# Attention and two MLPs on one core: late weight pairs in two parts beside the attention, the distance table's scaling behind a softmax, two sets of output tiles

## Chip, cores and metric

The kernel runs on one core of one Trainium2 chip. The metric is the device time of one launch in microseconds (us). Before the change it is 1016.96 us, the median of three runs (1013.14 to 1026.87). The profiled execution that all rows here come from took 1018.65 us, with a span of 1016.9 us inside it.

## What is computed

The reference is one attention layer with a learned bias on the distance, followed by two MLPs on all 2304 tokens (4 batches of 576). All data are float32.

```python
scores = q @ k.T / sqrt(64)                      # 4 batches, 8 heads, 576 x 576
x = log1p(abs(i - j)) / log1p(max(i, 1))         # the distance table
bias = relu(x * w1 + b1) @ w2                    # 32 hidden, one value per head
attn = softmax(scores + bias); a = attn @ v      # a: 2304 x 512
h = max(a @ w1, a @ w2, a @ w3)                  # first MLP, 512 -> 768
y = h @ w_out                                    # 768 -> 512
g = h2 if h2 >= 1 else 0 if h2 <= -1 else (h2 + 1)**2 / 4,  h2 = y @ w_in   # 512 -> 2048
out = g @ w_out2                                 # 2048 -> 512
```

## The kernel before

**Numbers.** Almost every product on TensorE (PE) is made of float16 halves: a float32 tensor is scaled by a power of two and split into a high and a low float16, and three products (high by high, high by low, low by high) are summed. So each weight has to be prepared once: the MLP weights come in as 64-bit floats, and `decode` (L457) turns a raw tile into float32 bits by two ScalarE (ACT) instructions (L462 writes a tile `z` from the high words, L463 writes `y` from the low words), one VectorE (DVE) instruction (L464, z = z shifted, or y) and one more ACT instruction (L465, a bfloat16 copy of |z| for the scale). `pair_scale` (L543) sums the columns of that copy over partitions with eight matmuls against ones on PE (L549) for a pair of tiles, and DVE takes the maximum and makes a power of two of it (L552, L136, L137, L141). `split` (L154) then writes the high half on ACT (L157) and the low half on DVE (L158). `decode` may be given a tile for z or, with None, makes z in place in the high words of the raw tile, that is with a step of two words; the first MLP's weights do so (L491), the late ones are given a tile of the pool `sp` (L579).

**Stages.** The work is cut into 144 slots, one for a block of 128 query rows, a batch and a head (or two heads for the short last block): 96 slots for the first three row blocks, then 48 in which the short block 4 and block 3 alternate for each batch. A slot is: the scores on PE (L691, into the pool `s` of two PSUM tiles), their sum with the bias and the row extreme on DVE (L705, into `sp`, a pool of four tiles), the exponential on ACT (L707), a float16 high half on ACT (L723), a low half on GpSimd (POOL; L724, L725, which end the use of the `sp` tile), a DMA transpose from SP's queue (L727), and three slots later the product with v on PE (L747, L743). A finished batch of a block is normalised (L756 to L762) and transposed into `xT` (L770). Between these, the main loop (L924) puts matmuls of the first MLP (mlp1, L802, with L807 and L809 on its results, and mlp2, L824) at a rate per slot, so that PE has work while a softmax runs. mlp2 scales its PSUM result into a tile of the pool `hl` on ACT (L829; two tiles), takes a maximum on DVE (L830) and stores it to DRAM from SP's queue (L831).

**Bias tables.** While a row block runs, the bias of the next is built in groups (L382 and L363): masks on DVE (L389, L369), matmuls (L393, L373), and a sum with the distance table. The distance table comes from DRAM by a DMA (L297, L302) at the start of a block, and `xscale` (L305) multiplies it by a column on DVE (L307). `new_xt` (L908) calls xscale at a table's first use; there are four such calls.

**Late weights.** The weights of the second MLP are the "late" pieces (L556): 16 pairs of tiles, by turns two of w_in and two of w_out, taken by a generator that is advanced by `late_to` (L538). Two advances make one pair: today all of the pair is done in the first one (the load of the next tile, both decodes, the load of the one after, the sums, the splits), and the second does nothing. The raw tiles of the first five pairs rotate over three places in `ws`, and tile x + 3 takes the place of tile x. During the last 48 slots the generator is advanced 0.3 times a slot (L983), up to ten advances, so five pairs (N_BIAS = 10 tiles) fall beside the attention; the others come after it, beside the rest of the first MLP.

**After the attention.** `wide` is set (L926) when the slots are at an end; from then on mlp1 and mlp2 may use the PSUM pool `s` too. The rest of the first MLP runs; then the second MLP for row block 0 (h2_mm L1041, g_mid L1047, out_mm L1067), beside which POOL prepares combinations of the output weights (wcomb L1096 to L1111); then the second MLP for the other blocks (h2_half L1119, g_pair L1125, out7 L1158) to the end.

**What sets the order.** The program is written in one order, and a scheduler reorders the instructions of each engine by priority and by its own estimate of the times, within the data's dependencies. `tc.issue_after(x)` forbids it to put an instruction ahead of x. `last_pair[0]` is the latest softmax's DVE instruction (L705) or, before the first softmax, the last bias instruction. On the chip each engine runs its instructions in the order that results, and so does SP's DMA queue.

Of the kernel before, what the change touches and what calls it, by code (L numbers as in the profile page):

```python
# [9 lines left out]
F32 = mybir.dt.float32  # L10
U32 = mybir.dt.uint32
# [9 lines left out]
def kernel(ctx: ExitStack, tc: tile.TileContext, qt, kt, vr, small, mw1, mw2, mw3, mwo, win, wo2, out):  # L21
# [8 lines left out]
    P = 128  # L30
    B, H, S, D = 4, 8, 576, 64
# [61 lines left out]
    def st(shape, dt, tag):  # L93
        return sb.tile(shape, dt, tag=tag, name=tag, bufs=BUFS.get(tag, 1))
# [59 lines left out]
    def split(hi, lo, src, scale, eng):  # L154

        if eng == "v":
            A.activation(hi, src, AF.Copy, scale=scale)  # L157
            V.scalar_tensor_tensor(lo, src, scale, hi, ALU.mult, ALU.subtract)  # L158
        else:
            G.tensor_tensor(src, src, (scale.unsqueeze(2) if len(src.shape) == 3 else scale).to_broadcast(src.shape), ALU.mult)  # L160
            A.activation(hi, src, AF.Copy)
            G.tensor_tensor(lo, src, hi, ALU.subtract)

    if True:
# [65 lines left out]
        wide, halves_left, turn = [], [], [0]  # L230
# [74 lines left out]
        def xscale(j, t):  # L305

            V.tensor_scalar(t, t, ipsi[:, j:j + 1], None, ALU.mult)  # L307
# [99 lines left out]
        last_pair = [None]  # L407
# [41 lines left out]
        def raw_load(src, r):  # L449
            SP.dma_start(r if len(src.shape) == 2 else r.rearrange("p (k f) -> p k f", k=src.shape[1]), src)  # L450
            return r
# [5 lines left out]
        def decode(r, z, y):  # L457

            w = r.bitcast(U32).rearrange("p (n two) -> p n two", two=2)
            if z is None:  # L460
                z = w[:, :, 1]
            A.activation(z.bitcast(F32), w[:, :, 1].bitcast(F32), AF.Prelu, scale=-(2.0 ** -80), alpha=-(2.0 ** -32))  # L462
            A.activation(y, w[:, :, 0], AF.Copy, scale=2.0 ** -29 * (1 - 2.0 ** -20), bias=-0.5)  # L463
            V.scalar_tensor_tensor(z, z, 3, y, ALU.logical_shift_left, ALU.bitwise_or)  # L464
            A.activation(high(y), z.bitcast(F32), AF.Abs)  # L465
            return z.bitcast(F32)

        def high(y):

            return y.bitcast(BF16)[:, 0:512]  # L470
# [55 lines left out]
        N_BIAS = 10  # L526

        def late_home(x):
            if x == 10:
                home[10] = st([P, S], F32, "xtab").bitcast(F16)[:, :1024]  # L530
            while len(home) <= x:
                home.append((st([P, S], F32, "k").bitcast(F16) if len(home) < 32 else st([P, 9, P], F16, "pt").rearrange("p c k -> p (c k)"))[:, :1024])
            return home[x]
# [22 lines left out]
        def late_pieces():  # L556

            spec = []
            for ft in range(0, NF2, 2):
                spec.append([win[:, P * f:P * f + P].rearrange("(k p) f -> p k f", p=P) for f in (ft, ft + 1)])  # L560
                spec.append([wo2[P * f:P * f + P, :] for f in (ft, ft + 1)])

            spec = sum(spec, [])

            def load(x):
                if x >= len(spec):
                    return
                r = [raws[:, 0], raws[:, 1], rt_.rearrange("p a c -> p (a c)").bitcast(I64)][x % 3]
                if x >= N_BIAS + 2 and x % 3 < 2:
                    r = st([P, 10, 256], F16, "v").rearrange("p a c -> p (a c)")[:, 0:2048].bitcast(I64)  # L570
                loaded.append(raw_load(spec[x], r))

            loaded = []
            load(0)
            load(1)
            for y in range(len(spec) // 2):
                load(2 * y + 2)
                dst = [late_home(2 * y + i) for i in range(2)]
                zs = [decode(loaded[2 * y + i], st([P, S], F32, "sp")[:, :512].bitcast(U32), dst[i].bitcast(U32)) for i in range(2)]  # L579
                load(2 * y + 3)  # L580
                q = y // 2
                s = c_sq2[:, q:q + 1] if y % 2 else c_sp[:, 2 * q:2 * q + 2]
                pair_scale(s, [d.bitcast(U32) for d in dst], 12 if y % 2 else 14)
                for i in range(2):
                    split(dst[i][:, 0:512], dst[i][:, 512:1024], zs[i], s[:, 0:1] if y % 2 else s[:, i:i + 1], PENG[y % 2])
                yield
                yield

        wo_done, n_wo = [], [0]
# [48 lines left out]
        def load(key):  # L638
            if key in kbox:
                return  # L640
            kind, j, b = key[:3]
            i0, n = BLK[j][0], BLK[j][1]
            if kind == "q":

                t = qz[:, key[3] % 4]
                if j == SJ:
                    for x in range(2):
                        p = slice(64 * x, 64 * x + 64)
                        G.memset(t[p, :, 64 - 64 * x:128 - 64 * x], 0.0)
                        SP.dma_start(t[p, :, p], qt[b, :, p, i0:i0 + n].rearrange("c p i -> p c i"))  # L650
                else:
                    SP.dma_start(t, qt[b, :, :, i0:i0 + n].rearrange("c p i -> p c i"))
            elif kind == "k":
                t = st([P, S], F32, "k")
                SP.dma_start(t, kt[b, key[3]])
            else:
                t = st([P, 10, 256], F16, "v")
                SP.dma_start(t, v_d[b, key[3]])
            kbox[key] = t
# [156 lines left out]
        def mlp2(key, d):  # L816
            while not wo_done:
                n_wo[0] += 1
                next(pieces, None)
            pm = mlp_ps()[:, :256]  # L820
            hh = hhs[:, order_of(key) % 2]
            for ft in range(NF1):
                for y, (wp, hp) in enumerate(SPLIT3):
                    T.matmul(pm, wo16[:, ft, wp, P * d:P * d + P], hh[:, ft, hp], start=(ft == 0 and y == 0), stop=(ft == NF1 - 1 and y == 2))  # L824
            t = st([P, 256], F32, "hl")
            bs = range(B) if key[0] == SJ else (2 * key[1], 2 * key[1] + 1)
            for x, b in enumerate(bs):
                c = slice(256 // len(bs) * x, 256 // len(bs) * (x + 1))
                A.activation(t[:, c], pm[:, c], AF.Copy, scale=c_rb[:, b:b + 1])  # L829
            V.tensor_reduce(c_xm[:, key[0], 4 * key[1] + d:4 * key[1] + d + 1], t, AX.X, ALU.max, apply_absolute_value=True)  # L830
            SP.dma_start(x2_d[key[0]][:, d, 256 * key[1]:256 * key[1] + 256], t)  # L831
# [74 lines left out]
        xts, scaled = {}, set()  # L906

        def new_xt(j):  # L908
            if j not in scaled:
                scaled.add(j)  # L910
                xscale(j, xts[j])
            return xts[j]

        early = {}
# [266 lines left out]
        for x in range(len(work) + GL):  # L1181
            if x < len(work):
                y, sub, ft = work[x]
# [17 lines left out]
            if x >= GL:  # L1201
                y, sub, ft = work[x - GL]
# [48 lines left out]
```

## Time and profile before

| | |
|---|---|
| median of three runs | 1016.96 us (1013.14 to 1026.87) |
| the profiled execution | 1018.65 us, span 1016.9 us |
| PE busy | 932.2 us of the span, 92% |
| DVE, ACT, POOL busy | 702.2, 600.9, 511.4 us |
| attention | ends about 557 us into the span |
| last 317 us | the second MLP, blocks 1 to 4 |

[...] In rows of a timeline, "[2.39 <-ACT ab L465]" says that the engine stood idle for 2.39 us before this instruction and that the ACT instruction of line 465, which wrote `ab`, ended the wait. [...]

### The profile page before, as it was taken

Reading aid. Unit: us, or ns where it says so; the run is one execution under the profiler, and the core shown is the slowest. Engines: PE = TensorE matmul, PEld = TensorE weight load, DVE = VectorE, ACT = ScalarE, POOL = GpSimd, SP = SyncE. Lnnn points to the kernel's source line nnn. Section 1 sums busy time; section 2 is a strip of 40 time slices with the busy share of each in tenths; the row PEclk is TensorE's granted clock in tenths of the full one; section 3 lists DMA queues with packets and bytes.
Section 4 is the critical chain, followed back from the end, with each engine's and each line's share of the span. In section 5 each row is a group of like instructions: output and inputs, shape, how many; then the busy total and the mean of one; then the engine's idle time right before and its main releaser. Section 6 shows DMA issues by size and latency. Waiting matters only on the chain. (4 is left out here: it accounts for less than half of the span.)

```text
span 1016.9 us, 25952 instructions
## 1 busy us (share of the span) xinstructions
PE 932.2 (92%) x10258; PEld 759.5 (75%) x10258; DVE 702.2 (69%) x1551; ACT 600.9 (59%) x1194; POOL 511.4 (50%) x734
## 2 busy tenths in 40 slices
PE   6776788899999999999889888989999999999996
PEld 5555668688888878777677777534588888888885
DVE  8976978777656686556455477886686686586565
ACT  4778975865666545778577689543344454444342
POOL 4131478666876755646357112977044343444442
PEclk9776969999999999999999999989999999999999
DMA  9877999999998979999989753010020010000000
GB/s 296 251 246 132 241 199 247 201 246 188 234 226 203 182 181 210 212 226 229 204 173 199 186 198 127 22 42 1 1 84 22 1 43 19 5 22 11 12 22 22
DMA packets 238970, 141.47 MB, mean 139 GB/s; under 512 B 187520, under 2 KB 217728, under 8 KB 238336
## 3 DMA queue, kind: packets, MB, share of 16 engines
q1 hardware_dynamic: 238688, 139.55, 58.3%
q8 instruction: 80, 1.31, 0.5%
q14 instruction: 42, 0.34, 0.1%
q10 hardware_dynamic: 160, 0.26, 0.1%
HBM read 79.68 MB, written 15.27 MB: 93 GB/s over the span
## 5 line engine op out<-in xcount | busy, mean ns | idle before, releaser
L802 PEld LDWEIGHTS <-aw 128*128 128x128 f16 x2160 | 190.0, 99 | 45.4 <-issue 23.4
L802 PE MATMUL pm<-xT,aw 128*128 128x256 f16 (+1 forms) x1812 | 202.7, 264 | 6.4 <-ACT hl L829 2.9
L725 POOL TENSOR_TENSOR phl<-sp,phl 128x512 f16<-128x512 f32 x136 | 161.6, 1189 | 0.0
L707 ACT ACTIVATE sp<-sp,mx 128x576 f32<-128x576 f32 x144 | 110.6, 768 | 69.9 <-DVE mx L705 69.4
L724 POOL TENSOR_TENSOR phl<-sp,phl 128x64 f16<-128x64 f32 x136 | 49.5, 364 | 179.2 <-ACT phl L723 145.6
L691 PE MATMUL s<-k,qz 64*128 64x288 f32 (+1 forms) x576 | 128.3, 460 | 10.4 <-DVE mx L705 7.9
L705 DVE CUSTOM_DVE_ANT_0 sp<-s,ab 128x576 f32<-128x576 f32 x128 | 93.2, 751 | 32.3 <-PE s L691 10.4
L1136 ACT ACTIVATE sp<-pm,vec 128x256 f32<-128x256 f32 x112 | 61.4, 556 | 81.2 <-PE pm L1119 78.1
L747 PEld LDWEIGHTS <-pt 128*128 128x128 f16 x1792 | 73.7, 101 | 30.5 <-DMA pt<-phl 20.3
L691 PEld LDWEIGHTS s<-k,qz 64*128 64x128 f32 (+1 forms) x576 | 70.4, 201 | 29.1 <-DVE mx L705 9.7
L723 ACT ACTIVATE phl<-sp 128x576 f16<-128x576 f32 x136 | 89.8, 672 | 3.5 <-DMA pt<-phl 2.6
L747 PE MATMUL pav<-v,pt 128*128 128x64 f16 x1568 | 72.1, 198 | 16.0 <-DMA pt<-phl 15.8
L1140 POOL TENSOR_TENSOR hh<-hh 128x128 f32<-128x128 f32 x56 | 33.0, 590 | 106.3 <-DVE hh L1138 90.2
L1119 PEld LDWEIGHTS <-ab 128*128 128x128 f16 x756 | 73.8, 98 | 9.2
L1137 DVE SCALAR_TENSOR_TENSOR hh<-pm,vec,sp 128x256 f32<-128x256 f32 x112 | 52.4, 477 | 33.5 <-ACT sp L1136 33.2
L824 PE MATMUL pm<-hh,wo 128*128 128x256 f16 x558 | 69.0, 273 | 2.6 <-POOL hh L814 1.0
L824 PEld LDWEIGHTS <-wo 128*128 128x128 f16 x648 | 61.0, 98 | 13.4 <-issue 6.1
L814 POOL TENSOR_TENSOR hh<-hm,hh 128x256 f16<-128x256 f32 (+1 forms) x60 | 44.8, 747 | 51.6 <-ACT hh L813 50.3
L1158 PEld LDWEIGHTS <-xT 128*128 128x128 f16 x588 | 57.5, 98 | 7.8 <-ACT xT L1145 1.2
L1158 PEld LDWEIGHTS <-wo 128*128 128x128 f16 x588 | 57.5, 98 | 6.7
L809 DVE SCALAR_TENSOR_TENSOR hm<-pm,hm 128x256 f32<-128x256 f32 (+1 forms) x108 | 41.9, 389 | 27.6 <-PE pm L802 10.6
L1141 POOL TENSOR_TENSOR hh<-hh 128x128 f32<-128x128 f32 x56 | 26.3, 470 | 68.5 <-DVE hh L1138 66.3
(300 smaller groups left out, 2004.4 us busy)
## 6 DMA issues: line engine op xcount, KB each, us to landing
k<-in_k_dram SPq DMA_DIRECT2D x64, 288.0 KB, 3.7
v<-v_d SPq DMA_DIRECT2D x24, 640.0 KB, 4.9
ws<-in_moe_w_out_dram SPq DMA_DIRECT2D x15, 512.0 KB, 5.0
ws<-in_moe_w_in_dram SPq DMA_DIRECT2D x9, 512.0 KB, 5.4
x_d<-hl SPq DMA_DIRECT2D x36, 128.0 KB, 2.5
qz<-in_q_dram SPq DMA_DIRECT2D x16, 256.0 KB, 5.0
ab<-in_moe_w_dram SPq DMA_DIRECT2D x8, 512.0 KB, 9.5
qz<-x_d SPq DMA_DIRECT2D x4, 1024.0 KB, 4.8
```

The source lines that it names most:

```text
L691: last_score[0] = T.matmul(sbox[i + r][:, c, :288], q[p, s if u.j == SJ else s // 2], k[p, 288 * c:288 * c + 288], start=True, stop=True)
L705: last_pair[0] = V.tensor_tensor_reduce(halves(sn), sbox.pop(i)[:, :, :288], halves(bias_sb[u.j][:, h]), -0.125, 3e38, ALU.add, ALU.min, mx)
L707: last_soft[0] = A.activation(pf, sn, AF.Exp, scale=-1.0, bias=mx, accum_out=u.sums[:, h:h + 1])
L723: A.activation(hl[:, :S], pf, AF.Copy)
L725: G.tensor_tensor(hl[:, S + 64:], pf[:, :512], hl[:, :512], ALU.subtract)
L747: T.matmul(u.pav[:, 64 * h:64 * h + 64], pt[:, c], v[:, sl, 64 * (h % 4):64 * (h % 4) + 64], **kw)
L802: T.matmul(o, wm[:, ft, i, wp, kk], x_rhs(key, xp, kk) if n == 256 else x_rhs(key, xp, kk)[:, c], start=(x == 0), stop=(x == 11))
L824: T.matmul(pm, wo16[:, ft, wp, P * d:P * d + P], hh[:, ft, hp], start=(ft == 0 and y == 0), stop=(ft == NF1 - 1 and y == 2))
L1119: T.matmul(pm, w[:, wp, kk], x2t[ORDER[y]][:, kk, xp, 256 * sub:256 * sub + 256], start=(x == 0), stop=(x == 11))
L1136: A.activation(r, pm, AF.Relu, scale=c_ch[:, f], bias=c_half)
L1137: V.scalar_tensor_tensor(t, pm, c_c[:, f], r, ALU.mult, ALU.max)
L1158: T.matmul(m[x], gl[:, gp, i], w[:, wp], start=(start and z == 0 and x % 2 == 0), stop=(stop and z == 2 and (x % 2 == 1 or x == 6)))
```

## The change

Three edits. First, in `late_pieces`, the pairs whose tiles all lie beside the attention (y = 0 to 4, `two`) are decoded in place, with no tile of `sp`, and are cut in two: the first advance makes the load of the next tile and the two decodes, the second makes the sums, the scale, the splits and then the load of the tile after, which used to come ahead of the sums. Since z now lies in the raw tile, that place is free for tile x + 3 only after the split has read it. Second, xscale is put after the latest softmax by `issue_after`. Third, while `wide` is set, every second output of mlp2 takes a tile of the pool `btmp` (two tiles, used in the bias stage and by `all_max`) in place of `hl`. The later lines move by 7, from L912 on by 8.

```diff
@@ late_pieces
             for y in range(len(spec) // 2):
                 load(2 * y + 2)
                 dst = [late_home(2 * y + i) for i in range(2)]
-                zs = [decode(loaded[2 * y + i], st([P, S], F32, "sp")[:, :512].bitcast(U32), dst[i].bitcast(U32)) for i in range(2)]
-                load(2 * y + 3)
+                two = 2 * y + 1 < N_BIAS
+                zs = [decode(loaded[2 * y + i], None if two else st([P, S], F32, "sp")[:, :512].bitcast(U32), dst[i].bitcast(U32)) for i in range(2)]
+                if two:
+                    yield
+                else:
+                    load(2 * y + 3)
                 q = y // 2
                 s = c_sq2[:, q:q + 1] if y % 2 else c_sp[:, 2 * q:2 * q + 2]
                 pair_scale(s, [d.bitcast(U32) for d in dst], 12 if y % 2 else 14)
                 for i in range(2):
                     split(dst[i][:, 0:512], dst[i][:, 512:1024], zs[i], s[:, 0:1] if y % 2 else s[:, i:i + 1], PENG[y % 2])
-                yield
+                if two:
+                    load(2 * y + 3)
+                else:
+                    yield
                 yield
@@ mlp2
-            t = st([P, 256], F32, "hl")
+            t = st([P, 256], F32, "btmp" if wide and d % 2 else "hl")
@@ new_xt
-                xscale(j, xts[j])
+                with tc.issue_after(last_pair[0].ins):
+                    xscale(j, xts[j])
```

PE's order around the second late pair, beside the attention. Before, the first four matmuls of the sum (L549) stand behind a product with v (L747) and ahead of the first MLP's matmuls (L802):

```order
L747 LDWEIGHTS pt
L747 MATMUL pav<-v,pt 128x64
L549 LDWEIGHTS ones
L549 MATMUL pm<-ab,ones 128x128
L549 LDWEIGHTS ones
L549 MATMUL pm<-ab,ones 128x128
L549 LDWEIGHTS ones
L549 MATMUL pm<-ab,ones 128x128
L549 LDWEIGHTS ones
L549 MATMUL pm<-ab,ones 128x128
L802 LDWEIGHTS aw
L802 MATMUL pm<-xT,aw 128x256
```

With the change, all eight stand together, behind that MLP work and one more pair of scores (L809 is the former L802; shown are the end of that work and the first two of the eight):

```order
L809 LDWEIGHTS aw
L809 MATMUL pm<-xT,aw 128x256
L809 LDWEIGHTS aw
L809 MATMUL pm<-xT,aw 128x256
L549 LDWEIGHTS ones
L549 MATMUL pm<-ab,ones 128x128
L549 LDWEIGHTS ones
L549 MATMUL pm<-ab,ones 128x128
```

Twelve such matmuls of the MLP stand between the last scores and the sum there, and two more rounds of twelve have moved ahead of it. The sum has gone from the place where its input has just been asked for to one about a slot later.

SP's queue near the end of the first late pair (names in brackets are the semaphores waited for; L450 is a load of a raw weight tile, L727 a transpose for the softmax, L770 one of a normalised block, L831 a store of mlp2). Before, both loads stand far up and wait for ACT, that is for the decodes:

```order
L658 DMA v<-v_d 128x2560 [waits PE_49]
L450 DMA ws<-in_moe_w_out_dram 128x512 [waits DMAHW7_49,Activation_49]
L655 DMA k<-in_k_dram 128x576 [waits DMAHW0_49,PE_49]
L450 DMA ws<-in_moe_w_in_dram 128x4x128 [waits DMAHW1_49,Activation_49]
L727 DMA_TRANSPOSE pt<-phl 128x9x128 [waits DMAHW2_49,Activation_49,Pool_49]
L770 DMA_TRANSPOSE xT<-px 128x8x128 [waits DMAHW3_49,Pool_49]
```

With the change (L734, L777, L662 and L838 are the former L727, L770, L655 and L831):

```order
L734 DMA_TRANSPOSE pt<-phl 128x9x128 [waits DMAHW0_49,PE_49,DMAHW6_49,Activation_49,Pool_49]
L777 DMA_TRANSPOSE masks<-px 128x4x128 [waits DMAHW7_49,Pool_49]
L450 DMA ws<-in_moe_w_out_dram 128x512 [waits DVE_49]
L662 DMA k<-in_k_dram 128x576 [waits DMAHW1_49,PE_49]
L450 DMA ws<-in_moe_w_in_dram 128x4x128 [waits DMAHW2_49,DVE_49]
L838 DMA x_d_75<-hl 128x256 [waits DMAHW3_49,Activation_49]
L734 DMA_TRANSPOSE pt<-phl 128x9x128 [waits DMAHW4_49,PE_49,Pool_49]
```

Both loads now wait for DVE, the split, and stand seven transposes (two of them of normalised blocks) and two loads of k lower.

DVE's order at the short block's distance table (`ws`). Before, its scaling stands in the middle of block 3's bias groups:

```order
L399 TENSOR_TENSOR btmp<-pm,xtab 128x256
L389 TENSOR_TENSOR masks<-rw,thr 128x1024
L400 SCALAR_TENSOR_TENSOR ab<-pm,vec,btmp 128x8x32
L307 TENSOR_SCALAR ws<-ws,vec 128x288
L389 TENSOR_TENSOR masks<-rw,thr 128x1024
L399 TENSOR_TENSOR btmp<-pm,xtab 128x256
```

With the change it stands directly ahead of its first use (L376), behind a softmax (L712, the former L705):

```order
L712 ISA sp,mx<-s,ab 128x576
L712 ISA mx 128x1
L307 TENSOR_SCALAR ws<-ws,vec 128x288
L816 SCALAR_TENSOR_TENSOR hm<-pm,hm 128x256
L369 TENSOR_TENSOR masks<-rw,thr 128x1024
L816 SCALAR_TENSOR_TENSOR hm<-pm,hm 128x256
L376 TENSOR_TENSOR btmp<-pm,ws 128x256
```

The first table's scaling moves in the same way, 88 rows down DVE's order, and between there and the end of block 1's bias groups the scheduler has dealt all engines a somewhat different order.

## Rows read from the trace of the kernel before

**Rows 1.** The page, part 1: span and busy time of each engine.

```profile
span 1016.9 us, 25952 instructions
PE 932.2 (92%) x10258; PEld 759.5 (75%) x10258; DVE 702.2 (69%) x1551; ACT 600.9 (59%) x1194; POOL 511.4 (50%) x734
```

**Rows 2.** Windows by stage: busy per engine, then granted clock, DMA share, GB/s.

```profile
260.00:400.00 140.00, 138.24 (x1943) 117.79 (x1942) 95.73 (x234) 82.44 (x201) 95.58 (x128) 1.00 0.96 205
400.00:560.00 160.00, 148.63 (x1894) 120.45 (x1893) 82.64 (x203) 114.04 (x249) 90.48 (x127) 0.98 1.00 208
560.00:650.00 90.00, 80.77 (x754) 67.64 (x751) 63.94 (x170) 67.22 (x138) 24.34 (x26) 1.00 0.47 145
650.00:700.00 50.00, 45.30 (x200) 19.86 (x199) 38.25 (x47) 23.06 (x36) 44.35 (x37) 0.93 0.09 29
700.00:1017.00 317.00, 307.49 (x2671) 260.91 (x2669) 214.05 (x418) 135.11 (x201) 121.79 (x230) 0.99 0.06 21
```

**Rows 3.** Timeline of PE: the sums of late pairs with an idle time.

```profile
415.88 0.38 PE L549 MATMUL pm<-ab,ones 128*128 128x128 bf16 x4 [0.68 <-ACT ab L465]
...
442.98 0.38 PE L549 MATMUL pm<-ab,ones 128*128 128x128 bf16 x4 [2.39 <-ACT ab L465]
...
511.36 0.38 PE L549 MATMUL pm<-ab,ones 128*128 128x128 bf16 x4 [3.40 <-ACT ab L465]
```

**Rows 4.** Timeline of ACT, 435 to 443 us: ahead of the second sum.

```profile
435.67 0.63 ACT L829 ACTIVATE hl<-pm,vec 128x128 f32<-128x128 f32 x2 [5.39 <-DMA x_d<-hl]
...
438.24 0.65 ACT L462 ACTIVATE sp<-ws 128x512 f32<-128x512 f32 x1
...
442.30 0.62 ACT L465 ACTIVATE ab<-sp 128x512 bf16<-128x512 f32 x1
```

**Rows 5.** Timeline of PE, one round of the first MLP's matmuls.

```profile
435.62 1.47 PE L802 MATMUL pm<-xT,aw 128*128 128x256 f16 x12
```

**Rows 6.** Windows of 5 us around the second and third stall.

```profile
440.00:445.00 5.00, 2.54 (x31) 1.98 (x30) 3.34 (x9) 5.00 (x13) 2.06 (x4) 0.86 0.96 300
445.00:450.00 5.00, 5.00 (x33) 3.94 (x32) 3.26 (x10) 3.70 (x8) 2.84 (x5) 0.80 1.16 289
510.00:515.00 5.00, 3.64 (x32) 2.99 (x32) 2.65 (x8) 4.53 (x12) 3.27 (x5) 0.69 0.79 221
515.00:520.00 5.00, 5.00 (x67) 4.15 (x65) 4.08 (x8) 3.35 (x7) 3.24 (x5) 0.97 0.90 130
```

**Rows 7.** Lines 464, 158, 157: duration ns min/median/max, first and last start.

```profile
L464 DVE SCALAR_TENSOR_TENSOR sp<-sp,ab x18: 680/692/1439, 413.2 to 591.5; 128x512 uint32<-128x512 uint32 x18
L464 DVE SCALAR_TENSOR_TENSOR ab<-ab,aw x8: 674/684/692, 36.6 to 124.1; 128x512 uint32<-128x512 uint32 x8
...
L158 DVE SCALAR_TENSOR_TENSOR ab<-sp,vec,ab x18: 736/746/1515, 420.8 to 604.1; 128x512 f16<-128x512 f32 x18
L158 DVE SCALAR_TENSOR_TENSOR aw<-ab,vec,aw x8: 739/777/1407, 65.4 to 140.8; 128x512 f16<-128x512 f32 x8
...
L157 ACT ACTIVATE ab<-sp,vec x18: 705/707/722, 420.0 to 603.3; 128x512 f16<-128x512 f32 x18
L157 ACT ACTIVATE aw<-ab,vec x8: 733/749/762, 60.1 to 136.9; 128x512 f16<-128x512 f32 x8
```

**Rows 8.** Tile ws: loads to landing; waits 460 to 500 us, the longest for a load.

```profile
DMA to landing us min/median/max: 3.6/5.9/11.4
...
ACT xtab L463 <- DMA ws<-in_moe_w_out_dram: 4.3, 1, 4.3
```

**Rows 9.** Timelines of DVE and PE, 224 to 228 us: the short block's table.

```profile
224.59 0.37 DVE L307 TENSOR_SCALAR ws<-ws,vec 128x288 f32<-128x288 f32 x1 [3.35 <-DMA ws<-log_d]
...
225.62 0.64 PE L393 MATMUL pm<-coef,masks 128*128 128x64 f16 x16 [0.84 <-DVE masks L389]
...
226.94 1.25 PE L824 MATMUL pm<-hh,wo 128*128 128x256 f16 x10 [0.62 <-DVE ab L400]
```

**Rows 10.** Timeline of PE after the attention: waits for an output's scaling.

```profile
604.84 1.47 PE L802 MATMUL pm<-xT,aw 128*128 128x256 f16 x12 [1.55 <-ACT hl L829]
...
611.29 1.47 PE L802 MATMUL pm<-xT,aw 128*128 128x256 f16 x12 [1.05 <-ACT hl L829]
```

**Rows 11.** Window of 130 to 150 us.

```profile
130.00:150.00 20.00, 18.00 (x163) 13.81 (x164) 13.68 (x29) 13.36 (x30) 16.21 (x20) 0.59 1.03 217
```

## Prediction

> **What bounds the kernel now.** I read the page's part on the engines first. PE is busy for 932.2 of 1016.9 us [rows 1], so whatever shortens the launch must take idle time or a slow clock out of PE's way. The windows by stage say where there is any [rows 2]. From 700 us to the end PE is idle for 9.5 us of 317, and the change touches nothing there; from 260 to 400 us for 1.8 of 140. In the last third of the attention, 400 to 560 us, it is idle for 11.4 of 160 us, and DVE and ACT have room (82.6 and 114.0 us). After the attention, 560 to 700 us, it is idle for 13.9 of 140.
>
> The timeline of PE gives the cause of those 11.4 us. Three times it stands before the first matmul of a late pair's sum, L549, and waits for ACT's L465, for 0.68, 2.39 and 3.40 us [rows 3]: 6.47 us. Before the second of these ACT had waited 5.39 us for a store of mlp2 to free a tile [rows 4], and only then did it come to the decodes; PE meanwhile ran out of what stands ahead of L549 in its order. Work that it could have done stood right behind: rounds of the first MLP, 12 matmuls in 1.47 us each [rows 5]. Both of the longer stalls also cost clock: in the windows of 440 to 450 us the granted clock is 0.86 and 0.80, of 510 to 520 us 0.69 and 0.97 [rows 6], that is 0.7 + 1.0 + 1.55 + 0.15 = 3.4 us of full-speed time, part of it while PE was idle anyway.
>
> **Edit 1, two parts.** It removes the wait at L549 by giving the sum a place about a slot later. PE's order shows it: in the second pair two rounds of 12 MLP matmuls, 2 x 1.47 = 2.9 us [rows 5], have moved ahead of the sum, longer than the stall of 2.39 us. They are work that has to be done in any case, so what they fill is gained. I count the idle time of the three stalls, 6.5 us. The upper bound adds the clock, 6.47 + 3.4 = 9.9 us. The lower is 0: the ACT wait for the store is still there [rows 4], and PE may come to rest at the next scores, which need the softmax behind that wait. I take 6.5, as the rounds in front cover most of each stall; the clock I leave out, because ACT's own stall remains.
>
> What it adds. In-place decoding reads and writes every second word. Ten tiles have one L464, one L158 and one L157 each. Lines that do this in the first MLP's weights stand in the trace beside those that don't: L464 684 against 692 ns, L158 777 against 746, L157 749 against 707 [rows 7]. That is 10 x (-8 + 31 + 42) = 0.65 us on DVE and ACT together, beside PE in a stretch where neither is full [rows 2]. Cost 0; without that cover 0.7 us.
>
> [...]
>
> It also frees two of the four `sp` tiles for each pair. It moves a load of each pair behind the split. On SP's queue it passes seven transposes and two loads of k in the first pair; these go out earlier, which costs nothing. Behind it now stand a store of mlp2 and the next transposes, and they would wait if SP came to it before the split is done; in the order shown SP comes to it after the short block's transpose. The load then has less time until its decode. The two advances lie 3.3 slots apart, 160 us / 48 slots x 3.3 = 11 us; the sums and the split take about 4 of them (the first pair's go from 415.88 us [rows 3] to a first L158 at 420.8 [rows 7]) and the landing 5.9 us in the median, 11.4 at most [rows 8]. About 1 us is left. Value 0; the bounds are 0 and the longest wait of a decode for its load today, 4.3 us [rows 8], in each of the four later pairs: 17 us, on ACT, with the exponentials queued behind.
>
> **Edit 2, the table's scaling.** Four DVE instructions change place. The third, today at 224.59 us, keeps DVE for 3.35 us because its DMA hasn't landed; behind it wait masks and sums of bias groups, and PE then stands for 0.84 and 0.62 us [rows 9]. It now goes next to its use, long after the DMA. That is worth 1.5 us at most and 0 at least; I take 1.0. The wait that it adds is for a softmax ahead of it on the same engine, so it can hold nobody up. But the first call's move makes the scheduler deal a different order to all engines up to the end of block 1's bias groups. I can't price that from rows, only bound it: today the window of 130 to 150 us has a clock of 0.59 [rows 11], 8.2 us of full-speed time lost, so such a stretch more or less is worth 8 us on either side. I take 0.
>
> **Edit 3, the second set of tiles.** It holds only after the attention. There PE waits twice for ACT's L829, 1.55 and 1.05 us [rows 10], but for ACT to come to it, not for a tile; the long waits for a store [rows 4] lie beside the attention, where `wide` is not set and nothing changes. Bounds 0 and 2.6 us of gain; I take 0. That the mlp2 of block 3 now stands ahead of the second MLP's first matmuls moves POOL and DVE between 650 and 700 us, where both are nearly full [rows 2]; I take 0 for that too.
>
> **Sum.** 1018.65 - 6.5 - 1.0 = 1011.2 us against the profiled execution. That lies 1.7 us above the median of 1016.96 us, so the same gains from the median would give 1009.5. I forecast 1011.
>
> **Rivals.** (a) *The stall only moves.* PE reaches the sum late but then rests at the scores, as softmax is what ACT's wait really delays. For it: two stalls follow an ACT wait of 5.4 us [rows 4] that stays. Against it: in the same stretches PE has MLP rounds it may take [rows 5]. Time: 1018.65 - 0.68 - 1.0 = 1017.
>
> (b) *The clock too.* Without gaps PE keeps 1.00 where it has 0.86, 0.80 and 0.69 today, as it does from 260 to 400 us, where it is 98% busy [rows 2, 6]. Time: 1018.65 - 9.9 - 1.5 = 1007.
>
> (c) *The load becomes the wait.* Slower than before: ACT stands at the decode of each pair's second tile because its load, now issued after the split, hasn't landed; exponentials wait behind, and the scores and products behind them. For it: about 1 us of slack against a landing that varies from 3.6 to 11.4 us [rows 8]. Against it: the scheduler knows the transfer and sets the second tile's decode later. It decides from 6.5 / 4 = 1.6 us of wait a pair; from there the gain is gone. At 4.3 us a pair: 1018.65 - 6.5 - 1.0 + 17 = 1028.
>
> (d) *No effect where it counts,* because the attention isn't the path: if the end were set by POOL from 650 to 700 us at its own pace, nothing earlier would show. But POOL's work there begins only when the weights and the first MLP are ready, so it moves with the attention's end. It gives 1018.65, and I put it with (a).
>
> **How the numbers follow.** Forecast 1011 (1006 to 1015): 0.50. Stall moves or no effect (1015 to 1020): 0.23. Clock too (1002 to 1007): 0.13. The load becomes the wait, or the early reorder goes the wrong way (1020 to 1032): 0.14. The range that holds it 8 times in 10 reaches from 1002 to 1022 us; it leaves out most of the last case and the luckiest end of the third. A measurement of this kernel tells about 2% from no change, 20 us: 997 and 1037. All cases but the far ends of the last two are inside: faster 0.04, same 0.93, slower 0.03.
>
> **What would show it.** Right: no idle time over 1 us before L549 between 400 and 560 us; a clock of 1.00 in that stretch; the attention's last product with v some 7 us earlier; no idle time before the short block's scaling; and from 700 us on the same lengths, only earlier. Wrong: idle time of the same size before the scores (for a); ACT waiting for `ws` loads at L462 or L463 by more than 1.6 us a pair (for c); a low clock anywhere from 60 to 250 us that isn't there today, which would be the early reorder.

## Result, and the profile after

The changed kernel took 1028.08 us in the median of four runs (1023.01 to 1028.41), the kernel before beside it 1015.05 (1011.25 to 1026.87): a ratio of 1.0110, 95% interval 1.0068 to 1.0151. That is within 2%, but slower, and outside the forecast range of 1002 to 1022 us. The profiled execution is the shortest of the four, 1023.01 us against 1018.65. Ratios here and below are of runs no more than 1.5% above the fastest of their own kernel, so a ratio can differ from that of the medians beside it.

Lines from 589 to 910 of the old numbering stand 7 lower in the changed kernel, later ones 8 (L549, L450 to L465 and L158 keep theirs). The page's part 1 and the windows by stage answer to [rows 1, 2]:

```profile
span 1021.2 us, 25951 instructions
PE 926.1 (91%) x10258; PEld 754.1 (74%) x10258; DVE 701.2 (69%) x1551; ACT 599.8 (59%) x1194; POOL 510.2 (50%) x734
```

```profile
260.00:400.00 140.00, 138.40 (x1930) 117.42 (x1929) 95.46 (x231) 80.47 (x197) 95.61 (x127) 1.00 0.95 207
400.00:560.00 160.00, 148.80 (x1908) 121.69 (x1905) 82.22 (x201) 114.24 (x251) 89.13 (x125) 0.98 1.01 210
560.00:650.00 90.00, 80.38 (x726) 66.19 (x727) 62.95 (x169) 65.74 (x137) 21.33 (x25) 0.98 0.43 138
650.00:700.00 50.00, 38.80 (x171) 16.81 (x169) 38.37 (x47) 21.97 (x33) 42.73 (x36) 0.93 0.08 27
700.00:1021.00 321.00, 313.19 (x2698) 263.58 (x2696) 215.22 (x419) 136.91 (x203) 123.62 (x232) 1.00 0.06 21
```

The stretch that was to gain, 400 to 560 us, has 11.2 us of idle PE where it had 11.4. The one that was to stay, 650 to 700 us, has 11.2 where it had 4.7. To see where time goes I cut each trace at three starts on the timelines: the 67th softmax (L705), the last softmax, and the first matmul of the second MLP's later blocks (L1119). Before: 289.4, 263.1 more, 175.4 more, and 289.0 to the end of the span. After: 287.8, 261.6, 183.0 and 288.8. So the trace gains 1.6 + 1.5 + 0.2 us and loses 7.6 between the last softmax and L1119, +4.3 in all (1021.2 - 1016.9).

In the attention the stalls at L549 [rows 3] are gone, none is over 0.45 us. The timelines of PE, ACT and DVE show what came instead:

```profile
436.80 1.24 PE L698 MATMUL s<-k,qz 128*128 128x288 f32 x4 [2.46 <-DVE mx L712]
...
484.86 1.49 PE L698 MATMUL s<-k,qz 128*128 128x288 f32 x4 [3.91 <-DVE mx L712]
...
509.85 1.67 PE L809 MATMUL pm<-xT,aw 128*128 128x256 f16 x13 [1.81 <-ACT hl L836]
...
435.00 0.63 ACT L836 ACTIVATE hl<-pm,vec 128x128 f32<-128x128 f32 x2 [6.55 <-DMA x_d<-hl]
...
435.65 0.42 DVE L837 TENSOR_REDUCE vec<-hl 128x1 f32<-128x256 f32 x1 [6.75 <-ACT hl L836]
...
482.19 0.67 ACT L462 ACTIVATE ws<-ws 128x512 f32<-128x512 f32 x1 [5.04 <-DMA ws<-in_moe_w_out_dram]
...
483.43 0.69 DVE L464 SCALAR_TENSOR_TENSOR ws<-ws,ab 128x512 uint32<-128x512 uint32 x1 [5.80 <-ACT ab L463]
...
504.28 0.67 ACT L463 ACTIVATE xtab<-ws 128x512 uint32<-128x512 uint32 x1 [4.40 <-DMA ws<-in_moe_w_out_dram]
```

PE now rests 2.46 and 3.91 us before scores and 1.81 us before the first MLP, 8.2 us against the 6.5 of [rows 3]. Ahead of each, ACT waits: once for a store, as in [rows 4], and twice for a load of a raw tile. The first two of these waits hold DVE too, with the next softmax (L712) behind it. Of the two waits for a load only that of 5.04 us is new; the kernel before waits 4.3 us at the same decode into `xtab` [rows 8].

After the attention, PE and DVE around the longest new wait (L1049 and L1075 are the former L1041 and L1067; L1063, L1064 and L1067 are the former L1055, L1056 and L1059 of g_mid):

```profile
652.21 2.75 PE L1075 MATMUL s<-ab,phl 128*128 128x512 f16 x12 [0.87 <-ACT btmp L836]
...
656.62 0.81 PE L1049 MATMUL pm<-ws,ab 128*128 128x512 f16 x3 [1.39 <-DVE sp L1063]
...
676.68 3.60 PE L1075 MATMUL s<-ab,phl 128*128 128x512 f16 x8 [8.32 <-DVE phl L1067]
...
662.83 0.74 DVE L1063 SCALAR_TENSOR_TENSOR sp<-pm,vec,sp 128x512 f32<-128x512 f32 x1
...
665.50 1.09 DVE L1025 TENSOR_SCALAR vec<-vec 128x16 f32<-128x16 f32 x1
666.51 1.28 DVE L158 SCALAR_TENSOR_TENSOR aw<-qz,vec,aw 128x512 f16<-128x512 f32 x1
667.72 1.12 DVE L141 TENSOR_SCALAR vec<-vec 128x16 uint32<-128x16 uint32 x1
668.75 2.68 DVE L158 SCALAR_TENSOR_TENSOR aw<-qz,vec,aw 128x512 f16<-128x512 f32 x1
...
672.04 2.35 DVE L158 SCALAR_TENSOR_TENSOR aw<-qz,vec,aw 128x512 f16<-128x512 f32 x2
674.31 1.12 DVE L1031 TENSOR_TENSOR vec<-vec 128x16 f32<-128x16 f32 x1
675.35 1.27 DVE L1067 SCALAR_TENSOR_TENSOR phl<-sp,vec,phl 128x512 f16<-128x512 f32 x1
```

PE stands for 8.32 us because DVE's L1067, which makes its input, stands behind the scaling and split of the next row block's input (split_x2: four L158 and small work on columns), which takes 10 us, from 665.5 to 675.35. In the kernel before the split stands behind the same fourth piece, but with that piece's phl (L1059) ahead of it, and PE waits less, though the split takes nearly as long there, 9.5 us from 662.85 to 672.34 (two rows of PE's timeline):

```profile
667.54 2.75 PE L1041 MATMUL pm<-ws,ab 128*128 128x512 f16 x12
674.84 3.15 PE L1041 MATMUL pm<-ws,ab 128*128 128x512 f16 x7 [4.54 <-DVE sp L1055]
```

### The profile page after: what moved, and what is told of

It reads as the page before. It is cut to its first block, busy times and chain, and to the rows that moved or that the text cites. A ratio compares the mean times of both kernels' runs of the same rounds, so it can differ in the third digit from the quotient of the medians.

```text
span 1021.2 us, 25951 instructions
## 1 busy us (share of the span) xinstructions
PE 926.1 (91%) x10258; PEld 754.1 (74%) x10258; DVE 701.2 (69%) x1551; ACT 599.8 (59%) x1194; POOL 510.2 (50%) x734
## 5 line engine op out<-in xcount | busy, mean ns | idle before, releaser
L809 PEld LDWEIGHTS <-aw 128*128 128x128 f16 x2160 | 191.9, 100 | 51.2 <-issue 27.3
L809 PE MATMUL pm<-xT,aw 128*128 128x256 f16 (+1 forms) x1812 | 204.0, 265 | 9.1 <-ACT hl L836 4.4
L698 PE MATMUL s<-k,qz 64*128 64x288 f32 (+1 forms) x576 | 123.6, 451 | 19.8 <-DVE mx L712 16.2
L712 DVE CUSTOM_DVE_ANT_0 sp<-s,ab 128x576 f32<-128x576 f32 x128 | 93.0, 751 | 31.0 <-PE s L698 17.1
L698 PEld LDWEIGHTS s<-k,qz 64*128 64x128 f32 (+1 forms) x576 | 66.6, 195 | 39.1 <-DVE mx L712 19.5
L754 PE MATMUL pav<-v,pt 128*128 128x64 f16 x1568 | 69.7, 197 | 13.5 <-DMA pt<-phl 13.5
L831 PE MATMUL pm<-hh,wo 128*128 128x256 f16 x558 | 69.2, 273 | 1.4 <-POOL hh L821 0.7
L831 PEld LDWEIGHTS <-wo 128*128 128x128 f16 x648 | 60.8, 98 | 12.7 <-issue 5.9
## 6 DMA issues: line engine op xcount, KB each, us to landing
ab<-in_moe_w_dram SPq DMA_DIRECT2D x8, 512.0 KB, 10.3
```

What stands on the lines that cost most here:

```text
L698: last_score[0] = T.matmul(sbox[i + r][:, c, :288], q[p, s if u.j == SJ else s // 2], k[p, 288 * c:288 * c + 288], start=True, stop=True)
L712: last_pair[0] = V.tensor_tensor_reduce(halves(sn), sbox.pop(i)[:, :, :288], halves(bias_sb[u.j][:, h]), -0.125, 3e38, ALU.add, ALU.min, mx)
L754: T.matmul(u.pav[:, 64 * h:64 * h + 64], pt[:, c], v[:, sl, 64 * (h % 4):64 * (h % 4) + 64], **kw)
L809: T.matmul(o, wm[:, ft, i, wp, kk], x_rhs(key, xp, kk) if n == 256 else x_rhs(key, xp, kk)[:, c], start=(x == 0), stop=(x == 11))
```

## Experiments

Theories at the start: the time is lost at the end, by edit 3's order after the attention (E); at the start, by edit 2's reordering (S); or in the attention, by edit 1's new waits (A). "Stretch" is the time from the last softmax to the first matmul of L1119, 175.4 us before; kernels that leave that part of the program alone show 175.3 to 175.8, so it tells single microseconds apart from one trace. The ratios do so only to some 3 us.

**Each edit alone, and two without the third** (the diffs are the three hunks above).

e1_only: 

> Edit 1 alone (late pairs in place and in two parts). Theory E (the end: edit 3's order after the attention costs the time): no loss here, 0 to -3 us against the kernel before, since the waits only move from L549 to the scores. Theory S (the start: edit 2's early reorder): the same, 0 to -3 us. Theory A (the attention: edit 1's new waits cost): +5 to +12 us, all of it between 400 and 560 us.

e2_only: 

> Edit 2 alone (the table's scaling behind a softmax). Theory S: +6 to +12 us, with a DVE or PE wait between 60 and 230 us that the kernel before doesn't have. Theories E and A: -2 to 0 us, the softmax of slot 53 at 244 to 246 us as in both traces so far.

e3_only: 

> Edit 3 alone (two sets of tiles for the first MLP's outputs after the attention). Theory E: +4 to +12 us, with PE idle 8 us or so before an output matmul of row block 0 between 650 and 700 us, where the kernel before has 4.54. Theories S and A: 0 us, within 2.

e12: 

> Edits 1 and 2 without edit 3. Theory E: the loss is gone, -4 to 0 us against the kernel before. Theory S or A: as slow as the whole change, +8 to +13 us.

| | ratio, 95% interval | median us | stretch us |
|---|---|---|---|
| e1_only | 1.0004 (0.9973 to 1.0035) | 1015.92 | 175.6 |
| e2_only | 1.0026 (0.9995 to 1.0057) | 1016.92 | 175.8 |
| e3_only | 1.0076 (1.0039 to 1.0113) | 1024.12 | 183.7 |
| e12 | 1.0042 (1.0015 to 1.0069) | 1019.99 | 175.3 |

At 1016 us these are +0.4, +2.6 and +7.7 us; their sum, 10.7, is near the whole change's 11.2. Theory E has most of it, S a quarter or more, A nothing that can be told from zero. Without edit 3, e12 keeps +4.3 us (1.5 to 7.0), between what E and what S and A expected. The trace of e3_only shows the same wait of 8.32 us, before the matmuls of L1067 in its own numbering.

**What in edit 3 costs.** Four variants of edit 3 or of its order, each on the kernel before:

```diff
 e3_pt:     t = st([P, 9, P], F16, "pt")...bitcast(F32) if wide and d % 2 else st([P, 256], F32, "hl")
 e3_not31:  "btmp" if wide and key != (3, 1) and d % 2 else "hl"
 e3_just31: "btmp" if wide and key == (3, 1) and d % 2 else "hl"
 ord_only:  (tile unchanged)
+           with tc.issue_after(last_mm[0].ins) if x == 0 else nullcontext():   # around the first h2_mm and g_mid
```

e3_pt: 

> Edit 3 alone, but every second output takes one of the softmax's transposed tiles (pt, idle by then) in place of btmp, which all_max also takes. Theory H (sharing btmp with all_max upsets the scale and split of row block 1): 0 to +2 us against before, the PE wait of 8.3 us before an L1067 back to 4.5. Theory O (all of block 3's mlp2 stands ahead of row block 0's first h2 matmul, so the second MLP starts later): +6 to +9 us, as edit 3 alone, with the first L1041 some 89 us behind the last softmax instead of 82. Theory P (GpSimd has hh ahead of the weight combinations): +6 to +9 us too.

ord_only: 

> The kernel before, with its old tiles; only row block 0's first h2 matmul is put behind the last mlp2 matmul of block 3, as edit 3 has it; GpSimd's order stays that of before. Theory O: +5 to +9 us. Theory H: 0. Theory P: 0.

e3_not31: 

> Edit 3 alone, but not for the last four outputs (block 3's second half), so btmp is free when row block 1's all_max comes; the first h2 matmul still stands behind block 3's mlp2. Theory H: 0 to +2 us. Theories O and P: +6 to +9 us.

e3_just31: 

> Edit 3 for the last four outputs alone; GpSimd's order is that of before, the first h2 matmuls stand behind two thirds of block 3's mlp2. Theory H: +6 to +9 us. Theory O: +3 to +8 us. Theory P: 0 to +2 us.

| | ratio, 95% interval | first L1041 after the last softmax | stretch us | PE idle in it | clock |
|---|---|---|---|---|---|
| before | | 82.3 | 175.4 | 15.8 | 0.98 |
| e3_only | 1.0076 (1.0039 to 1.0113) | 89.0 | 183.7 | 22.8 | 0.97 |
| e3_pt | 1.0022 (0.9988 to 1.0056) | 86.6 | 178.4 | 18.9 | 0.98 |
| ord_only | 0.9997 (0.9964 to 1.0031) | 87.1 | 176.1 | 18.1 | 1.00 |
| e3_not31 | 1.0034 (1.0001 to 1.0067) | 89.7 | 181.4 | 20.1 | 0.98 |
| e3_just31 | 1.0032 (1.0004 to 1.0060) | 91.1 | 179.2 | 15.4 | 0.96 |

The last two columns are from windows over the stretch, the idle time being its length less PE's busy time, the clock the granted one as a share of full speed:

```profile
552.47:727.88 175.41, 159.65 (x1177) 105.72 (x1175) 126.05 (x254) 106.16 (x199) 80.41 (x74) 0.98 0.31 95
...
549.18:732.89 183.71, 160.94 (x1177) 105.77 (x1175) 125.51 (x255) 106.33 (x199) 78.53 (x74) 0.97 0.30 91
...
550.24:729.49 179.25, 163.81 (x1177) 107.61 (x1175) 124.98 (x254) 106.21 (x199) 79.74 (x74) 0.96 0.31 93
```

(before, e3_only and e3_just31.) ord_only refutes theory O: its first h2 matmul comes 4.7 us later, and its runs and its stretch (0.7 us longer) are those of the kernel before. Theory H is not the whole: with pt in place of btmp 5.3 of the 8.3 us are gone, but PE's wait at L1067 is still 7.53 us, not 4.5, and e3_not31, which leaves btmp free for all_max, loses 6.0. Theory P stays open. The kernels with e3_only's order on GpSimd (e3_only, e3_pt, e3_not31) have 3.1 to 7.0 us more idle PE than before; ord_only, with GpSimd's order of before, has 2.3 more, and e3_just31, also with that order, none more. What e3_just31 loses is longer busy time of PE, 4.2 us, at a lower granted clock (0.96 against 0.98). So the loss goes with the orders that the scheduler deals once the outputs have more tiles, between 3.0 and 8.3 us by their details, and not with the tile or with that one place in PE's order alone; which engine's order carries it was not separated.

**Whether DVE's split is the place.** All variants still have split_x2 of block 1 after the fourth piece of row block 0, beside GpSimd's wcomb. Moved behind the twelfth:

```diff
-                    if ft == PRM["xat"] + 3:
+                    if ft == (12 if y == 0 else PRM["xat"] + 3):
                         split_x2(y + 1)
```

e3_x12 (with edit 3): 

> Edit 3 alone, with the scale and split of row block 1 (all_max and four L158 on DVE) moved from behind the 4th to behind the 12th output piece of row block 0, when GpSimd's weight combinations are over. Theory S (DVE, slowed beside GpSimd, is the bound there, and edit 3's order puts a phl of PE behind the split): PE's wait of 8.3 us at L1067 goes, the stretch from the last softmax to the end falls from 465 to 457 to 460 us, the time to 0 to +3 us against before. Theory F (the time is lost before, in the first MLP's last rounds, and the split only shows it): the stretch stays at 463 to 465 us, +6 to +8 us.

b_x12 (on the kernel before): 

> The kernel before with the same move of row block 1's split. Theory S: the wait of 4.5 us at L1041 goes, -3 to -5 us, the stretch from the last softmax to the end 452 to 454 us in place of 456.8. Theory F: 0, within 1 us, as a wait at another piece takes its place.

e3_x12: 0.9996 (0.9966 to 1.0025), stretch 174.4 us. b_x12: 0.9922 (0.9889 to 0.9955), 1010.75 us in the median, stretch 170.7 us. The waits of 8.32 and 4.54 us are gone, and behind 650 us none over 1.7 us takes their place. Windows of b_x12 (its granted clock from 650 to 700 us is 1.00, where it was 0.93 before) and its DVE at the moved split:

```profile
650.00:700.00 50.00, 47.41 (x219) 21.14 (x218) 32.25 (x32) 20.15 (x29) 47.12 (x40) 1.00 0.01 3
```

```profile
705.24 0.23 DVE L1017 TENSOR_SCALAR vec<-vec 128x16 f32<-128x16 f32 x1
...
705.81 0.75 DVE L158 SCALAR_TENSOR_TENSOR aw<-qz,vec,aw 128x512 f16<-128x512 f32 x1
...
706.55 0.75 DVE L158 SCALAR_TENSOR_TENSOR aw<-qz,vec,aw 128x512 f16<-128x512 f32 x1
707.21 0.17 DVE L1023 TENSOR_TENSOR vec<-vec 128x16 f32<-128x16 f32 x1
```

Behind the last of wcomb the same four L158 take 0.75 us each, where they took 1.2 to 2.7 (the line's view, before and b_x12):

```profile
L158 DVE SCALAR_TENSOR_TENSOR aw<-qz,vec,aw x4: 1276/1283/2619, 663.4 to 671.1; 128x512 f16<-128x512 f32 x4
...
L158 DVE SCALAR_TENSOR_TENSOR aw<-qz,vec,aw x4: 743/746/750, 705.8 to 708.0; 128x512 f16<-128x512 f32 x4
```

So the two waits are the split's, as theory S of these two runs has it. That edit 3's whole cost is the split's doesn't follow. In the stretch edit 3 costs 183.7 - 175.4 = 8.3 us with the split at its old place and 174.4 - 170.7 = 3.7 with it moved: 4.6 us go with the split, by one trace of each kernel. The runs can't tell this: by them edit 3 costs 0.9996 / 0.9922 = 1.0075 with the split moved and 1.0076 without, each with an interval of some 4 us on either side.

Of the 3.7 us the windows over the stretch, e3_x12 and then b_x12, show half as idle time of PE (14.4 against 12.6 us) and half as busy time (160.0 against 158.1 us, at a clock of 0.98 against 1.00 from 560 to 650 us):

```profile
550.23:724.67 174.44, 160.02 (x1177) 105.71 (x1175) 120.56 (x253) 105.00 (x198) 78.50 (x74) 0.99 0.31 95
...
548.91:719.64 170.73, 158.09 (x1177) 105.15 (x1174) 119.22 (x252) 105.15 (x198) 79.44 (x74) 1.00 0.32 97
```

Among the idle time are three waits of e3_x12 that b_x12 doesn't have:

```profile
652.26 2.75 PE L1067 MATMUL s<-ab,phl 128*128 128x512 f16 x12 [0.85 <-ACT btmp L829]
...
656.77 1.04 PE L1067 MATMUL s<-ab,phl 128*128 128x512 f16 x4 [0.68 <-ACT phl L1058]
...
659.39 1.90 PE L1067 MATMUL s<-ab,phl 128*128 128x512 f16 x8 [1.15 <-DVE phl L1059]
```

A longer wait that is no loss stands on the timeline of the changed kernel at the place of [rows 10]. PE waits there 2.56 us for L836, where it waited 1.55 and then 1.05 us: the two have become one.

```profile
604.17 1.79 PE L809 MATMUL pm<-xT,aw 128*128 128x256 f16 x12 [2.56 <-ACT hl L836]
```

None of what makes up the 3.7 us was tested by a run of its own.

**Edit 1: the cut or the late load.**

Against edit 1's code:

```diff
 e1_two: two parts, z in sp, load where it was
+                zs = [decode(..., st([P, S], F32, "sp")..., ...)]
+                load(2 * y + 3)
+                if two: yield
 e1_inpl: z in place, load behind the split, one part
                 zs = [decode(..., None if two else ..., ...)]
-                    yield
...
+                if two: load(2 * y + 3)
+                yield
```

e1_two: 

> Edit 1's cut in two parts alone: z stays in tiles of sp and the load of the next raw tile stays ahead of the sums; PE's order is nearly that of edit 1. If the late load took the gain back: ACT's waits of 5 us at L462 and L463 for a load between 455 and 510 us go, PE's stalls in the attention fall by 4 us or more, -3 to -6 us against before. If the stall only moves whatever the load does, or if the two sp tiles that are held longer stop the softmax: 0 to +5 us, with PE's waits at the scores.

e1_inpl: 

> Edit 1's decoding in place with the load behind the split, in one part as before. If the late load costs: ACT's waits for loads are longer than the 4.3 us of before, the stalls at L549 stay, +2 to +6 us. If it costs nothing: 0, within 2 us.

e1_two: 0.9953 (0.9924 to 0.9982). e1_inpl: 0.9997 (0.9968 to 1.0025). PE stays free of the stalls at L549 in e1_two and e1_only, while it waits there for 5.8 us in e1_inpl, by the tile view of `ws`. The decodes in place are hardly slower, 2.68 us a tile in e1_only against 2.63 before (medians of L462 to L465 added up), so the difference of e1_two and e1_only, 0.5%, is put down to the place of the load; the two also differ in the tile for z, and their intervals overlap a little. The tile view of `ws` from 400 to 560 us lists who waited, us and times; first before, then e1_only, then e1_two:

```profile
  ACT xtab L463: 4.3, 1
  ACT ab L463: 1.7, 1
```

```profile
  ACT ws L462: 7.2, 2
  ACT xtab L463: 5.4, 1
  ACT ab L463: 1.9, 1
```

```profile
  ACT xtab L463: 5.0, 1
  ACT ab L463: 2.1, 1
```

ACT waits 6.0 us for loads before, 14.5 in e1_only and 7.1 in e1_two; e1_inpl has 5.8 in the same view (without 0.2 at L465). So neither half of the edit is late alone: in one part the split follows the decode at once, and in two parts with own tiles the load doesn't wait for it. Together the load waits a slot longer. The expectation for e1_two was not met in every point: one wait of 5 us for a load remains (4.3 before), and its single trace has 10.3 us of idle PE from 395 to 560 us, as before (10.6, counting gaps over 0.45 us), so its gain rests on the runs.

**Edit 2: which table.** e2_late applies it with `if len(scaled) > 1`, e2_first with `if len(scaled) <= 1`.

e2_late: 

> Edit 2 for the third and fourth table only, so that the order up to 200 us stays that of before. If what edit 2 costs (some 3 us in its own run) lies in the reordered start: 0 to -1 us against before. If it lies at the short block's table: +2 to +4 us, and the time lost is seen between 220 and 400 us. If it costs nothing: 0.

e2_first: 

> Edit 2 for the first two tables alone; the third and fourth stay as in the kernel before. If the reordered start costs: +2 to +5 us. If edit 2 costs nothing: 0, within 2 us.

e2_late: 0.9964 (0.9927 to 1.0000), which is over eight of its twelve runs; the median of all twelve is 1016.66 us beside 1015.87, so it shows no gain. e2_first: 1.0051 (1.0022 to 1.0080). So the cost is at the reordered start. No single wait carries it, but the traces say where it lies. Up to the 67th softmax PE is idle for 52.1 to 53.5 us in the four traces with the new order at the start (the whole change, e2_only, e12, e2_first) and for 43.5 to 52.0 us in the sixteen others, 52.8 and 48.3 in the mean. Most of that is between the 30th and the 40th softmax, 8.7 to 9.4 us against 4.5 to 7.0; windows there of the kernel before and of e2_first:

```profile
143.45:194.76 51.31, 46.38 (x812) 40.61 (x811) 38.82 (x91) 33.37 (x82) 39.63 (x52) 0.90 0.88 198
...
140.77:185.81 45.04, 35.91 (x678) 31.22 (x677) 33.48 (x77) 26.17 (x66) 35.44 (x46) 1.00 0.89 181
```

The time of the 67th softmax itself doesn't show it: with the same order on all engines up to 540 us, traces reach it at times between 276.7 us (ord_only) and 292.3 us (e3_pt), which is more than what is sought.

**Tiles beside the attention, and sums of the gains.** hl_att takes btmp from slot 100 to the last slot and not afterwards; hl_x12 adds the moved split to it; two_x12 is e1_two with the moved split, two_x12_late adds e2_late.

hl_att: 

> The kernel before, with btmp as the second set of tiles for mlp2 beside the attention (from the 100th slot to the last) and not after it: the reverse of edit 3. Theory W (the store that frees hl is what delays ACT, and ACT's delay is PE's idle time there): ACT's waits of 5.39 and 5.47 us for a store go, PE's stalls at L549 fall from 6.5 to 1 us, -3 to -6 us. Theory M (PE's idle time only moves to the next late input, a load or a softmax): 0, within 2 us.

hl_x12: 

> Both the second set of tiles beside the attention (as in hl_att) and the split of row block 1 behind the 12th piece (as in b_x12). If the gains add: -9 to -12 us. If hl_att's gain of 2 us is only noise: -6 to -8 us. If it upsets the stretch behind the attention as edit 3 does: -3 to -6 us.

two_x12: 

> Two parts with the load where it was, and row block 1's split behind the 12th piece. If the two lie in separate stretches they add: -4.8 and -7.9 us, -11 to -14 us, a ratio of 0.986 to 0.990. If they overlap: -8 us, 0.992.

two_x12_late: 

> The same, and edit 2 for the third and fourth table only. If that part of edit 2 gives what was predicted: 1 us less than two_x12, which can hardly be told; if the short block's table costs: 2 to 4 us more.

hl_att: 0.9979 (0.9952 to 1.0007). Both ACT waits for a store are gone from its trace and so are the two stalls at L549 over 1 us, but PE then waits 4.02 us for a transpose (`pt`) at 439.70 us and has 10.1 us of idle time from 395 to 560 us (10.6 before, counted as above): theory M rather than W, though the interval reaches 4.9 us of gain. The tiles also change the order behind the attention: hl_att's stretch is 177.3 us, 1.9 longer than before, and hl_x12's 172.4, 1.7 longer than b_x12's. hl_x12: 0.9918 (0.9887 to 0.9949), no better than b_x12. two_x12: 0.9906 (0.9873 to 0.9939), two_x12_late: 0.9889 (0.9851 to 0.9927), 1006.19 us in the median of six runs against 1018.68 beside it. two_x12 falls short of the sum, 0.9875, and doesn't show how much of e1_two's gain is left beside the moved split: 0.9906 / 0.9922 is a gain of 0.2%, less than either interval's half-width. two_x12_late has the lowest ratio of all versions, but its interval overlaps those of two_x12, hl_x12 and b_x12.

## Why the prediction was wrong

- **Edit 3, "I take 0 for that too": the step that failed.** The prediction saw that mlp2 of block 3 would stand ahead of the second MLP and that POOL and DVE are nearly full from 650 to 700 us (44.35 and 38.25 of 50 us [rows 2]), and put the cost at nothing, with bounds on the side of a gain only. It was +7.7 us (4.0 to 11.5). In the trace PE waits 8.32 us for an input that has come to stand behind the split, where it waited 4.54; the split takes 10 us on a DVE that runs L158 in 1.21 to 2.68 us beside GpSimd's wcomb and in 0.75 without it. About half of the stretch's loss goes with that place of the split (4.6 of 8.3 us, one trace of each kernel); how the rest comes about stays open. A stretch in which two engines are nearly full and PE already waits 4.54 us was the place to give a bound of some microseconds upwards.
- **Edit 1, "I count the idle time of the three stalls, 6.5 us".** The stalls at L549 went, as predicted; the gain did not stay. Measured is +0.4 us (-2.7 to +3.6). Two rivals came together. The stall moved to the scores, as in (a), and the load became late, as in (c): ACT's waits for loads are 11.7 us in the changed kernel's view of `ws` (5.4, 4.4 and 1.9) against 6.0 before. The term "Value 0" for the load was the mis-sized one: with the load back in its place the cut in two gives 4.8 us (1.8 to 7.7), an interval that holds the 6.5. It rested on "about 1 us" of slack, which is less by its own rows: from 415.88 to 420.8 us are 4.9 us and not 4, so 0.2 us is left beside the median landing. The cost of decoding in place was small, as said: in the traces with it the medians are 692 to 694 ns for L464 (692 before) and 756 to 761 ns for most of L157 (707 before).
- **Edit 2, "I take 0" for the new order at the start.** +5.2 us (2.2 to 8.1) by e2_first, inside the bound of 8 that the text gave. The gain of 1 us at the short block's table can't be told from nothing: e2_late's ratio gives -3.7 us (-7.4 to 0), the medians of all its runs and of those beside it +0.8.
- **What would show it.** Right: no idle over 1 us before L549, no idle of DVE before the short block's scaling, and the same length from L1119 on (289.0 and 288.8 us). Wrong: the last softmax came 1.5 us earlier behind the 67th, and the last product with v 3.5 us earlier in the trace (563.3 against 566.8), not 7; the clock from 400 to 560 us stayed at 0.98.
- **The sum** had two gains of 7.5 us and no loss. With the terms as measured it is 0.4 + 2.6 + 7.7 = 10.7 us. Rival (c) came nearest, 1028 us, but by luck: the largest part is edit 3's, which (c) doesn't have.

## What to carry to other kernels

A second buffer is also a change of order: with the freed tile the scheduler deals other engines' instructions anew, and what that costs is to be looked for in PE's waits behind it, not at the tile. When a transfer is tied to a step and the step is cut and put off, the transfer goes with it; cut first, and move the transfer only if its next use is far. And a wait of 4.5 us that the profile already shows behind DVE, where L158 takes 1.28 us and more beside GpSimd and 0.75 without it, is a better first target than the rearrangement of stalls in a stretch that has three inputs nearly late: moving that split, one line, gave 7.9 us (4.6 to 11.3) by the ratio, 5.1 by the medians and 4.7 in the stretch.

## What the runs showed of the hardware

Beside GpSimd's wcomb DVE was slower, which the prediction gave no price, and not in all its instructions. L158, with two inputs in SBUF, took 0.75 us in b_x12, where GpSimd stands still (the last instruction of wcomb ends at 699.14 us), and 1.21 to 2.68 us beside wcomb in the changed kernel; a TENSOR_TENSOR on 16 columns 0.17 us (L1023 of b_x12) and 1.12 beside it (L1031); a TENSOR_SCALAR on 16 columns, with one input in SBUF, 0.23 us (L1017 of b_x12) and 1.09 beside it (L1025). L1063, which reads one input from PSUM, took 0.74 us beside it and its like 0.75 without it (L1055 of b_x12 at 701.15 us). What makes the difference between these instructions no run here shows.

Equal orders don't make equal starts. ord_only and e3_pt, whose instructions stand in the same order on every engine until after the attention, reach the 67th softmax 15.6 us apart. Their windows up to there differ in the granted clock, 0.91 and 0.87:

```profile
0.00:276.70 276.70, 233.24 (x3195) 191.53 (x3196) 219.76 (x521) 196.91 (x419) 158.19 (x219) 0.91 0.97 234
...
0.00:292.30 292.30, 242.26 (x3195) 199.65 (x3196) 221.43 (x521) 198.34 (x419) 156.84 (x218) 0.87 0.94 223
```

At these clocks 24.9 and 38.0 us of full-speed time are lost, 13.1 us of the difference. PE is busy 9.0 us longer and idle 6.6 us longer; what starts it the traces don't show. The spread is as large as the effects sought here, so a stretch that begins behind it (175.3 to 175.8 us wherever its code is the same) tells more than the whole time of one trace.
